# Four small edits in a kernel for delta attention and two gated layers: two more weight loads ahead of a marked point, one matrix product moved in the order, the last copies cut in two, one table load moved

## The chip, the cores and the metric

The kernel runs on one core of a Trainium2 chip. The metric is the device time of one execution in microseconds (us); lower is better. TensorE is written PE here (PEld for its weight loads), VectorE is DVE, ScalarE is ACT, GpSimd is POOL, SyncE is SP. L934 means line 934 of the kernel before.

## The reference

Three stages, one after the other, all in float32 (the inputs of the two layers come as float64 and are read as pairs of 32-bit words):

```python
# attention: q, k, v of (4, 8, 768, 48), beta of (4, 8, 768); a state of 48 x 48 for each head
for t in range(S):
    y[:, :, t] = q_t @ state
    state += beta_t * outer(k_t, v_t - state.T @ k_t)       # k_t normalised
x = y.transpose(0, 2, 1, 3).reshape(3072, 384)
# layer 1, d_ff = 1536
g = x @ w_gate
x = (g * sigmoid(g) * (x @ w_val)) @ w_out
# layer 2, d_ff = 2048
h = x @ w_in
out = np.where(h > 0, h, exp(min(h, 0)) - 1) @ w_out
```

## The kernel before

**Attention** is done in 12 groups g of 256 tokens. For a group SP loads k, q and v (`loads`: L447, L453, L460), `prepare` normalises k, makes transposes and products of k and q, and `invert` solves a small triangular system with many short DVE instructions (L673, L679) that end in a transpose (L687). `attention` then makes products on PE: `xstep` (L772, evicted by `xput`, L777), `gstep` (L792, evicted by `put`, L801), the chain over the state (L828) and the output (L862), transposed into `xh` and `xl` (L892, L895), the two parts of the input to layer 1.

**Layer 1** (`moe1`) runs over 12 blocks f of 128 columns for each group. A block is two projections on PE (L1028; gate, then value), Silu of the gate on ACT (`silu`, L1035), a product on DVE (L1038), its split into two parts (`hi` on ACT, L1042; `lo` on DVE, L1045) and the output product (`prod`, L1054), summed in `acc`. Results go through memory (`x2d`) to layer 2.

**Layer 2** (`moe2`) runs over 6 pairs of groups n and 16 blocks f each. A block is the projection `h2` (L1140, nine products), then `e0` Relu, `e1` Exp and `e2` on ACT (L1146, L1149, L1152), `e3`, `hi` and `lo` on DVE (L1155, L1160, L1163), then `out2` for four token tiles t (L1177), three products each. Tiles t = 0 and 1 are summed in the two halves of `acc`, t = 2 and 3 in two further banks (`at`). After the last block of a pair `ev` copies each tile out of its bank (L1190; even t on DVE, odd t on ACT) and `snd` issues its store on SP (L1194).

**Weights.** Layer 1 has 18 weight tiles w0 to w17: w0 and w1 hold gate and value columns of f = 0 and f = 1, w2 the output rows of both, w3 and w4 the columns of f = 2 and 3, w5 their rows, and so on. `load_w` issues one tile as two or four transfers on SP (L934 for columns, L931 for rows; 786,432 bytes a tile). `decode` turns a tile into two float32r parts in six passes over 128x768: `lowbits` (L954, ACT), `mag` (L960, ACT), the sign (`sign16` on ACT, L965, or `sign32` on DVE, L968, whichever the planner gives it to), `both` (L972, DVE), `hi` (L982, ACT) and `lo` (L986, DVE).

**The order** of all instructions is made by a planner (`Order`) when the program is built. Every step has costs for the engines that can do it, a priority (a lower number goes first) and the steps that it follows; the planner plays the program through and writes each engine's queue in the order of its own times. On the chip an engine takes its queue strictly in order and waits only where data or a buffer is not ready. Step `after=` is only a rule for the planner. A weight tile's load has priority 1 + n and the loads of the second group have 2.5. From tile number AHEAD on, a load may be planned only behind `mark[PAUSE]`, which is the last `xput` of the first group:

```python
load_w(n, src1(n), 1 + n, [] if n < AHEAD else [mark[PAUSE], sent[n - 2]])
```

Where the planner sees PE without work before its time 170 us, it puts in products that nothing reads: `fill` (L1207, 128x512), `quick` (L1213) and, in layer 1, `fill2` (L1218, 128x256). `h2` of a block has priority f within its pair, `out2` has f + 2, so that `h2` of block f + 1 precedes `out2` of block f, and `out2` of block f precedes `h2` of block f + 2.

Of the kernel before, what the change touches and what calls it, by code (L numbers as in the profile page):

```python
# [245 lines left out]
def delta_moe_kernel(ctx: ExitStack, tc: tile.TileContext, q, k, v, beta,  # L246
# [14 lines left out]
    ND = 10  # L261
    UNTIL = 170e3
    JOIN = (4,)
    AHEAD = 3
    PAUSE = (0, 'x')
    HOLD = (0, 'm')
    WARM = 8
# [72 lines left out]
    def act(n, f, psum=True):  # L340
        return [("ACT", (75 if psum else 110) + .8333 * n, (165 if psum else 190) + .8333 * n, 0, f)]
# [4 lines left out]
    def pe(ns, f, kind=0, n=18):  # L346
        return [("PE", ns, ns + 160, (kind, n), f)]
# [10 lines left out]
    P_MOE = 0.0  # L358
# [649 lines left out]
    def moe1(g, p):  # L1008
        xk = [("xh", g % 2, 0), ("xh", g % 2, 1), ("xl", g % 2, 0), ("xl", g % 2, 1),
              f"xh{g % 2}", f"xl{g % 2}"]  # L1010
        ev = None
        for f in range(F1):
            m, o = divmod(f, 2)
            wk = [f"w{3 * m + o}", f"w{3 * m + o}b"]
            ok = [f"w{3 * m + 2}", f"w{3 * m + 2}b"]
            h, hh = Slots(GV, 1), Slots(HB, 1)
            ht = Slots(TBS, 1)
            c = {}

            def proj(j, f=f, h=h):  # L1020
                def x():
                    dst = bank[h.got[0]][:, j * TB:(j + 1) * TB]
                    wt = w1(f, j)
                    n = 0
                    for a_, b_ in PASS:
                        xx = (xh, xl)[b_][g % 2]
                        for kk in range(KD):
                            PE.matmul(dst, lhsT=wt[:, a_, kk * 128:(kk + 1) * 128], rhs=xx[:, kk, :],  # L1028
                                      start=(n == 0), stop=(n == 3 * KD - 1))
                            n += 1  # L1030
                return x

            def silu(h=h, ht=ht, c=c):
                c['s'] = TT(ht.got[0], [128, TB])
                A.activation(out=c['s'], in_=bank[h.got[0]][:, 0:TB], func=ACTF.Silu)  # L1035

            def times(h=h, c=c):
                V.tensor_tensor(out=c['s'], in0=bank[h.got[0]][:, TB:2 * TB], in1=c['s'], op=ALU.mult)  # L1038

            def hi(hh=hh, c=c):  # L1040
                c['h'] = TT(hh.got[0], [128, 2, TB], F32R)
                A.copy(out=c['h'][:, 0, :], in_=c['s'])  # L1042

            def lo(e, c=c):
                return lambda: e.tensor_tensor(out=c['h'][:, 1, :], in0=c['s'],  # L1045
                                               in1=c['h'][:, 0, :].bitcast(F32), op=ALU.subtract)

            def prod(f=f, c=c):
                od.fill = fill2
                w = w1(f, 2)  # L1050
                for n, (a_, b_) in enumerate(((0, 0), (1, 0), (0, 1))):
                    for d in range(KD):
                        o_ = acc[:, d // 2, (d % 2) * TB:(d % 2) * TB + TB]
                        PE.matmul(o_, lhsT=w[:, a_, d * 128:(d + 1) * 128], rhs=c['h'][:, b_, :],  # L1054
                                  start=(f == 0 and n == 0 and d != 1), stop=(f == F1 - 1 and n == 2),
                                  skip_group_check=True)
            pp = p + f
            mark.setdefault((g, 'm'), add(pp, pe(1080, proj(0), 1), r=xk + wk, w=[(h, 0)], need=[h]))
            add(P_MOE, act(256, silu), r=[(h, 0)], w=[ht], need=[ht], use=[h])
            add(pp, pe(1080, proj(1), 1), r=xk + wk, w=[(h, 1)], use=[h])  # L1060
            add(P_MOE, dve(256, times), r=[(h, 1)], w=[ht], use=[h])
            after = buf.get(('evac', g - 1), ()) if f == 2 else ()
            add(P_MOE, act(256, hi, False), r=[ht], w=[(hh, 0)], need=[hh], use=[ht], after=after)
            add(P_MOE, dve(256, lo(V)), r=[ht, (hh, 0)], w=[(hh, 1)], use=[ht, hh])
            add(pp + 1.5, pe(1080, prod, 1), r=[(hh, 0), (hh, 1)] + ok, w=["acc"], use=[hh])
        buf['evac', g] = []
        for d0, d1 in ((0, 2), (2, KD)):
            h = Slots(HB, 1)
            c = {}

            def take(d0=d0, d1=d1, h=h, c=c):
                c['t'] = TT(h.got[0], [128, d1 - d0, TB])
                A.copy(out=c['t'], in_=acc[:, d0 // 2, 0:(d1 - d0) * TB].rearrange(
                    "p (d t) -> p d t", t=TB))

            def send(d0=d0, d1=d1, c=c):
                nc.sync.dma_start(out=x2d[g, :, d0:d1, :], in_=c['t'])
            buf['evac', g].append(add(P_MOE, act((d1 - d0) * TB, take), r=["acc"], w=[h], need=[h]))
            add(0, dma(131072 * (d1 - d0), send), r=[h], w=[("x2d", g, d0)], use=[h])
# [47 lines left out]
    def moe2(n, f, p, obs):  # L1127
        h, hr = Slots(H4, 1), Slots(HB, 1)
        tag = ("kp", "qp", "ain")[cnt["hs"] % 3]
        cnt["hs"] += 1  # L1130
        c = {}
        wk = [f"w{f}", f"w{f}b"]
        xk = [(x, n % 2, d) for x in ("x2h", "x2l") for d in range(KD)]

        def h2():
            x = bank[h.got[0]]
            m = 0
            for a_, b_ in PASS:
                for kk in range(KD):
                    PE.matmul(x, lhsT=W[f][:, 0, a_, kk * 128:(kk + 1) * 128], rhs=x2[n][b_][:, kk, :],  # L1140
                              start=(m == 0), stop=(m == 3 * KD - 1))
                    m += 1

        def e0():
            c['r'] = TT(hr.got[0], [128, TB2])
            A.activation(out=c['r'], in_=bank[h.got[0]], func=ACTF.Relu, scale=-1.0)  # L1146

        def e1():
            A.activation(out=c['r'], in_=c['r'], func=ACTF.Exp, scale=-1.0)  # L1149

        def e2():
            A.activation(out=c['r'], in_=c['r'], func=ACTF.Identity, bias=neg1, scale=1.0)  # L1152

        def e3():
            V.scalar_tensor_tensor(out=c['r'], in0=bank[h.got[0]], scalar=0.0, in1=c['r'],  # L1155
                                   op0=ALU.max, op1=ALU.add)

        def hi():
            c['h'] = TT(tag, [128, 2, TB2], F32R)
            V.tensor_copy(c['h'][:, 0, :], c['r'])  # L1160

        def lo():
            V.tensor_tensor(out=c['h'][:, 1, :], in0=c['r'], in1=c['h'][:, 0, :].bitcast(F32),  # L1163
                            op=ALU.subtract)
        add(p, pe(2100, h2, 1), r=xk + wk, w=[h], need=[h],
            after=buf['evac', NB - 1] if n == 0 and f > 1 else ())
        add(P_MOE, act(512, e0), r=[h], w=[hr], need=[hr], use=[h])
        add(P_MOE, act(512, e1, False), w=[hr])
        add(P_MOE, act(620, e2, False), w=[hr], r=["neg1"])
        add(P_MOE, dve(512, e3), r=[h], w=[hr], use=[h])  # L1170
        add(P_MOE, dve(256, hi), r=[hr], w=HS[tag], use=[hr])
        add(P_MOE, dve(512, lo), r=[hr] + HS[tag], w=[(tag, "lo")], use=[hr])
        for t in range(4):
            def out2(t=t):
                o = bank[obs[t].got[0]][:, 0:DM]
                for m, (a_, b_) in enumerate(PASS):
                    PE.matmul(o, lhsT=c['h'][:, b_, t * 128:(t + 1) * 128], rhs=W[f][:, 1][:, a_, :],  # L1177
                              start=(f == 0 and m == 0), stop=(f == F2 - 1 and m == 2))
            add(p + 2, pe(530, out2, 1, 6), r=wk + HS[tag] + [(tag, "lo")], w=[obs[t]],
                need=[obs[t]] if f == 0 else [], wait=["acc"] if n == 0 and f == 0 else [])  # L1180
        if f == F2 - 1:
            for t in range(4):
                ot = ("xh1", "xl1", "y0", "y1")[cnt["os"] % 4]
                cnt["os"] += 1
                ok = [ot] + ([(ot[:2], 1, 0), (ot[:2], 1, 1)] if ot[0] == "x" else [])
                d = {}

                def ev(t=t, ot=ot, d=d):
                    d['o'] = TT(ot, [128, DM])
                    (A.copy if t % 2 else V.tensor_copy)(out=d['o'], in_=bank[obs[t].got[0]][:, 0:DM])  # L1190

                def snd(t=t, d=d):
                    r0 = t * S + n * 128
                    nc.sync.dma_start(out=out[r0:r0 + 128, :], in_=d['o'])  # L1194
                add(P_MOE, (act if t % 2 else dve)(384, ev), r=[obs[t]], w=ok, use=[obs[t]])
                add(0, dma(196608, snd), r=ok)

# [104 lines left out]
```

## Time and profile before

| | |
|---|---|
| median of 3 runs | 1166.56 us (1163.58 to 1168.1) |
| profiled execution: its time, its span | 1167.36 us, 1165.7 us |
| mean granted clock of PE, share of full speed | 0.985 |
| PE busy | 1123.9 us, 96% of the span |
| DVE, ACT, POOL busy | 812.3 us (70%), 560.8 us (48%), 44.3 us (4%) |

The profile is one execution; all times in it count from the start of its span. A busy PE also counts the products that nothing reads.

### The profile page before, as it was taken

The page shows a single profiled execution, that of the slowest core. Times are in us where ns is not written, and L with a number is a line of the kernel's source. Part 1 is how long each engine was busy: PE and PEld are TensorE (multiplying, and loading weights), DVE is VectorE, ACT ScalarE, POOL GpSimd, SP SyncE. Part 2 cuts the span into 40 slices and gives each one's busy share as a digit, 9 for nine tenths or more (in the row PEclk, how much of TensorE's full clock was granted, in tenths as well). Part 3 has the DMA queues.
Part 4 walks back from the last instruction along what each step waited for, and adds up shares of the span by engine and source line. Part 5 has one row for each costly group of instructions (what it writes and reads, how often), then busy time and mean ns, then how long its engine had stood idle before and what let it go on. Part 6 is the DMA issues. An engine that isn't in the chain of part 4 may idle for free.

```text
span 1165.7 us, 34386 instructions
## 1 busy us (share of the span) xinstructions
PE 1123.9 (96%) x14728; PEld 1032.0 (89%) x14728; DVE 812.3 (70%) x2489; ACT 560.8 (48%) x1099; POOL 44.3 (4%) x57
## 2 busy tenths in 40 slices
PE   8889999999999999999999999999999999999997
PEld 6689988989899989998999898988888888888886
DVE  7889867878887878788878765995545444454443
ACT  7688442333333333334333434995545454454443
POOL 0100010100000000000000000000000000000000
PEclk9799999999999999999999999999999999999999
DMA  7770202020202020203020105900101001010000
GB/s 156 235 214 16 43 14 45 11 49 8 50 9 50 9 50 9 50 5 54 9 50 6 26 3 168 334 15 19 55 1 55 1 14 42 1 37 1 28 1 28
DMA packets 107625, 57.36 MB, mean 49 GB/s; under 512 B 77744, under 2 KB 102320, under 8 KB 107472
## 3 DMA queue, kind: packets, MB, share of 16 engines
q1 hardware_dynamic: 107472, 55.16, 17.9%
q8 instruction: 115, 1.88, 0.7%
q14 instruction: 38, 0.31, 0.1%
HBM read 45.71 MB, written 9.44 MB: 47 GB/s over the span
## 4 chain that ended last, share of the span: by engine, by line
PE 80%; DVE 12%; ACT 4%; issue 3%; DMA 0%; POOLq 0%; DVEq 0%; ACTq 0%
PE gv L1028 24%; PE acc L1054 10%; PE acc L1177 8%; PE at L1177 8%; PE at L1140 8%; PE gv L1140 8%; PE at L828 2%; PE at L792 2%; PE at L772 2%; PE at L598 1%; PE at L557 1%; PE acc L1207 1%; DVE hb L1045 1%; PE at L862 1%; DVE ain L642 1%
## 5 line engine op out<-in xcount | busy, mean ns | idle before, releaser
L1028 PE MATMUL gv<-xh,w 128*128 128x256 f32 x1728 | 291.5, 289 | 5.9 <-ACT xh L892 2.4
L1028 PEld LDWEIGHTS gv<-xh,w 128*128 128x128 f32 x1728 | 242.5, 194 | 12.2 <-ACT xh L892 3.1
L1054 PE MATMUL acc<-hb,w 128*128 128x256 f32 x1296 | 183.5, 287 | 1.2 <-ACT hb L1042 0.6
L1054 PEld LDWEIGHTS acc<-hb,w 128*128 128x128 f32 x1296 | 165.6, 192 | 5.0 <-ACT hb L1042 1.2
L1035 ACT ACTIVATE tb<-gv 128x256 f32<-128x256 f32 x144 | 55.3, 384 | 233.6 <-PE gv L1028 233.2
L1028 PE MATMUL gv<-xl,w 128*128 128x256 f32 x864 | 152.8, 286 | 3.3 <-DVE xl L895 3.2
L1028 PEld LDWEIGHTS gv<-xl,w 128*128 128x128 f32 x864 | 125.9, 194 | 4.4 <-DVE xl L895 4.0
L1038 DVE TENSOR_TENSOR tb<-gv,tb 128x256 f32<-128x256 f32 x144 | 60.3, 419 | 67.1 <-ACT tb L1035 54.7
L1042 ACT CAST hb<-tb 128x256 fp32r<-128x256 f32 x144 | 58.6, 407 | 87.9 <-DVE tb L1038 87.6
L1155 DVE SCALAR_TENSOR_TENSOR hb<-gv,hb 128x512 f32<-128x512 f32 x48 | 33.2, 691 | 94.3 <-ACT hb L1152 94.3
L1155 DVE SCALAR_TENSOR_TENSOR hb<-at,hb 128x512 f32<-128x512 f32 x48 | 33.2, 691 | 82.6 <-ACT hb L1152 82.6
L657 DVE TENSOR_TENSOR ain<-z,ain 128x60 f32<-128x60 f32 (+32 forms) x522 | 88.7, 208 | 2.5
L664 DVE TENSOR_TENSOR z<-z,ain 128x60 f32<-128x60 f32 (+32 forms) x522 | 88.7, 208 | 1.0
L1045 DVE TENSOR_TENSOR hb<-tb,hb 128x256 fp32r<-128x256 f32 x144 | 65.5, 455 | 14.7 <-ACT hb L1042 13.7
L1146 ACT ACTIVATE hb<-gv 128x512 f32<-128x512 f32 x48 | 28.7, 599 | 97.2 <-PE gv L1140 97.1
L1152 ACT ACTIVATE hb<-hb,neg 128x512 f32<-128x512 f32 x96 | 69.5, 724 | 3.0
L1146 ACT ACTIVATE hb<-at 128x512 f32<-128x512 f32 x48 | 28.7, 598 | 80.1 <-PE at L1140 79.8
L1149 ACT ACTIVATE hb<-hb 128x512 f32<-128x512 f32 x96 | 60.8, 633 | 2.9
L792 PE MATMUL at<-gr,R 32*96 32x80 f32 x1480 | 46.4, 255 | 1.0 <-issue 1.0
L792 PEld LDWEIGHTS at<-gr,R 32*96 32x96 f32 x1480 | 38.7, 163 | 7.8 <-ACT tb L1035 0.8
L1177 PE MATMUL acc<-w,ain 128*128 128x384 f32 x192 | 39.7, 340 | 1.7 <-DVE ain L1160 1.3
L1177 PE MATMUL acc<-w,kp 128*128 128x384 f32 x192 | 39.5, 339 | 1.6 <-DVE kp L1160 1.3
(209 smaller groups left out, 2090.0 us busy)
## 6 DMA issues: line engine op xcount, KB each, us to landing
w<-in_moe_w_out_dram SPq DMA_DIRECT2D x28, 384.0 KB, 6.7
w<-in_moe_w_in_dram SPq DMA_DIRECT2D x16, 384.0 KB, 5.8
w<-in_moe_w_gate_dram SPq DMA_DIRECT2D x12, 384.0 KB, 7.4
w<-in_moe_w_val_dram SPq DMA_DIRECT2D x12, 384.0 KB, 7.8
qp<-in_q_dram SPq DMA_DIRECT2D x11, 384.0 KB, 5.8
kp<-in_k_dram SPq DMA_DIRECT2D x11, 384.0 KB, 5.2
x2d<-hb SPq DMA_DIRECT2D x12, 256.0 KB, 2.0
R<-in_v_dram SPq DMA_DIRECT2D x24, 96.0 KB, 2.2
```

The source lines that it names most:

```text
L657: V.tensor_tensor(out=t, in0=z[:, l:l + 1, x:y].to_broadcast([128, m, y - x]), in1=an[:, l + 1:32, l:l + 1].to_broadcast([128, m, y - x]), ...
L664: V.tensor_tensor(out=z[:, l + 1:32, x:y], in0=z[:, l + 1:32, x:y], in1=t, op=ALU.add)
L792: PE.matmul(bank[h[c].got[0]][0:96, s * 80:s * 80 + 80], lhsT=R[t, u, :], rhs=gr[t, u, 0:80], start=True, stop=True, skip_group_check=True)
L1028: PE.matmul(dst, lhsT=wt[:, a_, kk * 128:(kk + 1) * 128], rhs=xx[:, kk, :], start=(n == 0), stop=(n == 3 * KD - 1))
L1038: V.tensor_tensor(out=c['s'], in0=bank[h.got[0]][:, TB:2 * TB], in1=c['s'], op=ALU.mult)
L1045: return lambda: e.tensor_tensor(out=c['h'][:, 1, :], in0=c['s'], in1=c['h'][:, 0, :].bitcast(F32), op=ALU.subtract)
L1054: PE.matmul(o_, lhsT=w[:, a_, d * 128:(d + 1) * 128], rhs=c['h'][:, b_, :], start=(f == 0 and n == 0 and d != 1), stop=(f == F1 - 1 and n ...
L1140: PE.matmul(x, lhsT=W[f][:, 0, a_, kk * 128:(kk + 1) * 128], rhs=x2[n][b_][:, kk, :], start=(m == 0), stop=(m == 3 * KD - 1))
L1149: A.activation(out=c['r'], in_=c['r'], func=ACTF.Exp, scale=-1.0)
L1152: A.activation(out=c['r'], in_=c['r'], func=ACTF.Identity, bias=neg1, scale=1.0)
L1155: V.scalar_tensor_tensor(out=c['r'], in0=bank[h.got[0]], scalar=0.0, in1=c['r'], op0=ALU.max, op1=ALU.add)
L1177: PE.matmul(o, lhsT=c['h'][:, b_, t * 128:(t + 1) * 128], rhs=W[f][:, 1][:, a_, :], start=(f == 0 and m == 0), stop=(f == F2 - 1 and m == 2))
```

## The change

Four edits. (1) AHEAD goes from 3 to 5: w3 and w4 may be planned ahead of the marked point. (2) In layer 1, behind the Silu of the last block of the last group, ACT gets an Exp of a 128x1 tile whose result is not used, planned at 1400 ns. (3) `h2` of the last block of the last pair gets a priority lower by 0.5, so that it precedes `out2` of block 13. (4) In the last pair each tile's copy out of its bank is two copies of 192 columns, the first on DVE and the second on ACT, and the store follows both.

```diff
-    AHEAD = 3
+    AHEAD = 5
...
             add(P_MOE, act(256, silu), r=[(h, 0)], w=[ht], need=[ht], use=[h])
+            if g == NB - 1 and f == F1 - 1:
+                add(P_MOE, [("ACT", 1400.0, 1500.0, 0, lambda: A.activation(
+                    out=sm[2][:, 0:1], in_=neg1, func=ACTF.Exp))], r=["neg1", ht], w=["sm"])
...
-        add(p, pe(2100, h2, 1), r=xk + wk, w=[h], need=[h],
+        add(p - (0.5 if n == NB // 2 - 1 and f == F2 - 1 else 0), pe(2100, h2, 1), r=xk + wk, w=[h], need=[h],
             after=buf['evac', NB - 1] if n == 0 and f > 1 else ())
...
-                def ev(t=t, ot=ot, d=d):
-                    d['o'] = TT(ot, [128, DM])
-                    (A.copy if t % 2 else V.tensor_copy)(out=d['o'], in_=bank[obs[t].got[0]][:, 0:DM])
+                parts = 2 if n == NB // 2 - 1 else 1
+                w_ = DM // parts
+                for x in range(parts):
+                    def ev(t=t, x=x, ot=ot, d=d, w_=w_):
+                        if x == 0:
+                            d['o'] = TT(ot, [128, DM])
+                        (A.copy if (t if parts == 1 else x) % 2 else V.tensor_copy)(
+                            out=d['o'][:, x * w_:x * w_ + w_], in_=bank[obs[t].got[0]][:, x * w_:x * w_ + w_])
+                    e = (act if (t if parts == 1 else x) % 2 else dve)
+                    add(P_MOE, e(w_, ev), r=[obs[t]] + (ok if x else []), w=[("o", t, x)] + ([] if x else ok),
+                        use=[obs[t]])
...
-                add(P_MOE, (act if t % 2 else dve)(384, ev), r=[obs[t]], w=ok, use=[obs[t]])
-                add(0, dma(196608, snd), r=ok)
+                add(0, dma(196608, snd), r=ok + [("o", t, x) for x in range(parts)])
```

## Rows read from the trace of the kernel before

**Rows 1.** Page, part 1: busy time, share of span, instructions.

```profile
PE 1123.9 (96%) x14728; PEld 1032.0 (89%) x14728; DVE 812.3 (70%) x2489; ACT 560.8 (48%) x1099; POOL 44.3 (4%) x57
```

**Rows 2.** Busy time by stretch; columns: stretch, length, engines, PE clock, DMA share, GB/s.

```profile
15.00:20.00 5.00, 5.00 (x62) 3.93 (x62) 4.35 (x20) 3.73 (x6) 0.00 (x0) 1.00 1.03 268
20.00:25.00 5.00, 3.50 (x146) 2.81 (x148) 4.59 (x16) 5.00 (x5) 0.00 (x0) 0.93 0.01 2
...
24.00:58.00 34.00, 28.88 (x785) 22.69 (x774) 28.53 (x52) 23.31 (x41) 3.50 (x3) 0.76 0.73 212
58.60:125.00 66.40, 62.56 (x1232) 58.45 (x1230) 62.05 (x125) 54.62 (x92) 3.88 (x3) 0.97 0.37 100
```

**Rows 3.** The same for L1218 alone (products nothing reads), 0 to 180 us, the sum.

```profile
sum 180.00, PE 7.09 PEld 6.31; mean PE 0.20 PEld 0.18
```

**Rows 4.** Chain that ended last, 78 to 93 us: start, length, what.

```profile
80.61 0.91 ACT w L954
81.53 0.84 ACT w L982
```

**Rows 5.** Timeline of SP: start, length, line, tile and source, count.

```profile
25.79 0.38 SPq L447 DMA_DIRECT2D kp<-in_k_dram  x1
26.22 1.30 SPq L934 DMA_DIRECT2D w<-in_moe_w_gate_dram  x1
```

**Rows 6.** Waits of SP, 0 to 150 us: total us, times, longest.

```profile
SPq L447 <- DVE gr L546: 13.0, 1, 13.0
```

**Rows 7.** Timeline of PE around the first group's xstep.

```profile
33.96 0.76 PE L772 MATMUL at<-gr,ain 32*32 32x80 f32 x25 [3.52 <-issue]
```

**Rows 8.** Waits of DVE, 24 to 58 us.

```profile
DVE gr L777 <- PE at L772: 1.9, 2, 1.0
DVE lc L801 <- PE at L792: 1.0, 2, 0.8
DVE w L986 <- ACT w L982: 1.0, 1, 1.0
```

**Rows 9.** Instructions of L968 on DVE: times in ns (min/median/max), first and last start.

```profile
L968 DVE SCALAR_TENSOR_TENSOR w<-w x25: 942/951/960, 48.4 to 782.1; 128x768 int32<-128x768 int32 x25
```

**Rows 10.** Timeline of ACT, 72 and 86 us: Silu of blocks 3 and 4.

```profile
72.29 0.39 ACT L1035 ACTIVATE tb<-gv 128x256 f32<-128x256 f32 x1
...
86.87 0.39 ACT L1035 ACTIVATE tb<-gv 128x256 f32<-128x256 f32 x1 [0.48 <-PE gv L1028]
```

**Rows 11.** Chain that ended last, 750 to 765 us.

```profile
756.77 0.75 ACT hb L1073 x2
...
757.54 1.28 ACT L1149
...
758.83 0.64 ACT hb L1149
```

**Rows 12.** Waits of PE, 740 to 800 us.

```profile
PE acc L1177 <- DVE kp L1160: 1.3, 1, 1.3
```

**Rows 13.** ACT by form: copy of 192 columns, function of one column.

```profile
L840 ACT COPY sv<-at 48x192 f32<-48x192 f32 x3 | 0.9, 317 | 0.1
L1227 ACT ACTIVATE sm<-neg 128x1 f32<-128x1 f32 x1 | 0.2, 203 | 0.0
```

**Rows 14.** Timeline of PE from 1155 us.

```profile
1157.81 0.44 PE L1177 MATMUL acc<-w,ain 128*128 128x384 f32 x1 [1.26 <-DVE ain L1160]
1158.54 1.14 PE L1177 MATMUL acc<-w,ain 128*128 128x384 f32 x5 [0.28 <-DVE ain L1163]
```

**Rows 15.** Instructions of L1190, the whole run, and who waited.

```profile
  DVE xh L1190: 5.7, 6
```

**Rows 16.** Timeline from 1159 us: copies and stores.

```profile
1159.72 0.56 DVE L1190 COPY xh<-acc 128x384 f32<-128x384 f32 x1 [1.23 <-PE acc L1177]
...
1160.77 0.48 ACT L1190 COPY y<-at 128x384 f32<-128x384 f32 x1
1161.24 0.91 SPq L1194 DMA_DIRECT2D out_dram<-y  x2
```

## Prediction

> **What bounds the kernel now.** I read the page's first part, then busy time by stretch, then the chain of waits in the three places that the diff touches. PE is busy 96% of the span and DVE 70% [rows 1], so as a whole PE sets the time, and an edit on DVE or ACT pays only where PE is idle or turns products that nothing reads. There are three such places. From 58.6 to 125 us, while the 18 weight tiles of layer 1 are decoded, PE is idle for 66.40 - 62.56 = 3.8 us and spends 7.1 us on `fill2`, while DVE is busy 62.05 of 66.40 us: DVE is the bound there [rows 2, 3]. The chain of waits says with what: passes of `decode` [rows 4], and Silu of block 3 comes at 72.3, that of block 4, which needs w6, only at 86.9 [rows 10]. The second place is the start of layer 2, where PE waits 1.3 us for the first `out2` [rows 12]. The third is the end: behind `out2` of block 14 PE waits 1.26 and 0.28 us for the split of block 15 [rows 14].
>
> **Edit 1, AHEAD.** It adds and removes no instruction; it moves transfers. First what the pause is: on SP nothing waits for the last `xput`. w3 is issued at 26.22, right behind k of group 2 (counting from 1), and it is this k load that stood for 13.0 us, until DVE had read the old k [rows 5, 6]; `xput` is later, since its products end after 33.96 [rows 7]. So the queue becomes: w0 to w4 with no wait, then q and k of the second group, then w5 and w6 at about 26.2, where w3 and w4 were. q goes out later by four issues; nobody reads it before the k of its group, which stands behind the same wait as before. Five transfers of 786 KB then run into the quiet stretch: DMA moves 268 GB/s from 15 to 20 us and 2 GB/s from 20 to 25 [rows 2]; two tiles at 268 GB/s are 1.57 MB / 268 = 5.9 us, so w3 lands near 22 to 23 and w4 near 25.5. That costs the path nothing visible: what hides it is that DMA had 5 us without work. The 3.52 us in which PE waits for nothing that the profile shows lie beside the transfers issued at 26.2 [rows 5, 7]; w5 and w6 now take that place, so I leave the stall.
>
> What comes of it: `decode` of w3 and w4 can start some 20 us earlier than now, when the first of its sign passes on DVE is at 48.4 [rows 9]. A tile wants two or three passes of 0.951 us on DVE, so the two tiles 3.8 to 5.7 us. In 24 to 58 us DVE has 34 - 28.5 = 5.5 us free [rows 2]. Not all of that holds a pass: three waits are 1.0 us long, and one 0.8 [rows 8]. I take three passes, 2.9 us. Bounds: 0, if the planner's own times show no gap there, and 5.5 us, all that is free. Below 0 it goes too (the rival further down). What DVE does early it needn't do after 58.6, where it is the bound, and PE has 3.8 + 7.1 = 10.9 us of idle time and unread products to give up. So -2.9 us.
>
> **Edit 2, the table.** The load is 1.28 us between a copy that ends at 757.52 and the first Exp at 758.83 [rows 11], on the chain to the first `out2`, for which PE waits 1.3 us [rows 12]. Moved up to the last Silu it comes before work of lower priority (three decode passes), which then stands behind it; ACT has no gap there, so the load is not hidden by idle time, only exchanged with those passes. The added Exp of one column is 0.2 us, by the row of the Sqrt of that shape [rows 13]. Bounds: -1.3 (the wait is gone) and +0.2 (the planner pushes everything back by the load, and the passes still go first). I take -1.1, near the first, since products of layer 1 and 2 have priority 0 on ACT and decode has 500 and more. If the passes pushed back are late for block 3 of layer 2, part comes back; that is in the bound.
>
> The Trainium skill (ScalarE: Activation LUTs, What ACT_TABLE_LOAD costs) puts a switch at 1283 ns for the load and some 1380 ns of drain, 2.66 us in all. By it this edit would give up to 2.5 us, and the sum would be 1.4 us lower. The trace agrees on the load and shows no drain: from the end of the copy to the first Exp are 1.31 us.
>
> **Edit 3, `h2` of block 15.** PE's order at the end is now `h2` 14, `out2` 13, `h2` 15, `out2` 14, wait, `out2` 15. It becomes `h2` 14, `h2` 15, `out2` 13, 14, 15. The chain of block 15 on ACT and DVE starts 2.1 us earlier (one `out2` of four tiles), and I take both engines to be free for it: ACT is busy 48% and DVE 70% of the span [rows 1]. The product before the wait ended at 1157.81 - 1.26 = 1156.55; the bulk of the last `out2` starts at 1158.54 with one product of twelve done [rows 14]. Without the wait it starts at 1156.55 and has twelve: 1158.54 - 1156.55 = 2.0 us less. Bounds: 0 (the planner's times keep the old order) and -2.1 (all of one `out2`). I take -2.0.
>
> **Edit 4, the copies.** Now the last copy is 0.48 us on ACT at 1160.77, and the two last stores are issued from 1161.24 [rows 16]. A copy of 192 columns on ACT is 0.32 us [rows 13]; DVE's 0.56 cut in the same ratio is 0.37. Two halves at once would end the last copy some 0.1 us earlier. But they read one bank. In all six pairs ACT's copy from `acc` sat until DVE's copy from `acc` had ended (5.7 us in six times), and those were even two banks of one tile [rows 15]. So the halves go in turn: for t = 0 and 1 a chain of 0.37 + 0.32 + 0.37 + 0.32 and hops, 1.45 us from 1159.7; then t = 2 and 3, whose last half ends near 1161.8 instead of 1161.25. SP's spacing of about 0.45 us between stores hides half of that. Bounds: -0.1 and +0.6. I take +0.3.
>
> The Trainium skill (PSUM — Partial Sum Buffer, PSUM bank collisions raise a hardware error) says that two engines, ACT and DVE too, must not touch one bank in the same quadrant of partitions at once, and that accesses there are kept apart; different banks run clean. It speaks against this edit. By it only the halves of one tile go in turn, which gives +0.2 in the place of +0.3; the trace shows the turn even between the two banks of `acc`.
>
> **The sum**, against the profiled execution of 1167.36 us (1165.7 of span and 1.7 around it): -2.9 - 1.1 - 2.0 + 0.3 = -5.7, so 1161.7. That execution lies 0.8 us above the median, so the median becomes 1166.56 - 5.7 = 1160.9 us, 0.49% less. Its own range: 1158.5 to 1163.
>
> **Rivals.** (A) Edit 1 gives nothing: the planner sees no gap ahead of 58 us, or PE's stalls move elsewhere. For it: DVE's gaps are there because PE stood for 3.52 us [rows 7, 8], and the planner may not know of that stall. Against: ACT has 34 - 23.3 = 10.7 us free there [rows 2]. It gives -2.8, 1163.8 us. (B) Edit 1 gives all that DVE has free, 5.5 us, or more, if block 4 moves up in the place of `fill2` and PE's clock, 0.97 in that stretch [rows 2], no longer dips: -5.5 - 2.8 = -8.3, 1158.3 us; PE's 10.9 us give the far end, 1152.9. For it: block 4 waits 14 us for w6 [rows 10]. Against: half of DVE's gaps are shorter than a pass. (C) Slower: the twelve passes of w3 and w4 stand in ACT's and DVE's queues ahead of the first group's copies, and a queue goes in order, so that a pass that waits for its weights to land, or that has just begun, holds `xput`, `put` and the state's chain behind it, and PE, which idles meanwhile, has its lower clock for longer (0.76 of full speed in 24 to 58 us [rows 2], 1.2 GHz being half). Twelve passes of 0.9 us [rows 4, 9], all on the path, are +10.8 - 2.8 = +8.0, 1174.6 us; from ten passes on (+9.0 - 2.8 = +6.2) it is slower by over 0.5%. Against: the 3.52 us stall covers the first three or four.
>
> **Chances.** A time within 0.5% (5.8 us) of before can't be told from no change here, as the three runs before already differ by 0.4%. The forecast sits on that bound: 0.40, of it 0.21 beyond it. A 0.24 (within). B 0.23 (faster). C 0.13: 0.10 slower, 0.03 within, when fewer than ten passes are on the path. Faster 0.21 + 0.23 = 0.44, same 0.19 + 0.24 + 0.03 = 0.46, slower 0.10. The range leaves out the far end of B (0.08) and most of C (0.11): 1155.0 to 1167.0.
>
> **What would show it.** Edit 1: SP issues five tiles before the k load of 25.8 us; `lowbits` of w3 before 26 us; Silu of block 4 well before 86.9; less than 7.1 us of L1218. It is wrong if `xput` or the first Silu of layer 1 come later by more than 3 us. Edit 2: a table load near 752 at L1060 or so, none at 757.5, and no wait of 1.3 us at the first `out2`. Edit 3: two projections in a row at the end and no wait at the last `out2`. Edit 4: the ACT halves begin when the DVE halves end. The total is wrong if PE's idle time between 125 and 740 us changes by more than 3 us, for the planner writes that stretch anew as well, and nothing in the diff says which way.

## The result and the profile after

The changed kernel takes 1143.53 us (median of 6 executions, 1140.05 to 1148.89), the kernel before beside it 1163.11 (6 executions, 1160.88 to 1168.1). The ratio is 0.9833 (95% interval 0.9806 to 0.9860): 19.6 us less, where the forecast had 5.7 and its range reached down to 1155. The profiled execution took 1148.89 us, the slowest of its six.

Part 1 of the page of the changed kernel, which answers to [rows 1]:

```profile
PE 1116.3 (97%) x14711; PEld 1027.4 (90%) x14711; DVE 808.2 (70%) x2489; ACT 562.0 (49%) x1104; POOL 43.3 (4%) x57
```

The span fell by 1165.7 - 1147.2 = 18.5 us: PE's idle time from 41.8 to 30.9 us, its busy time by 7.6. Where that lies is seen best when the span is cut at three marks, the first Silu of the second group, the last Silu of layer 1, and the end:

| | to first Silu of group 2 | from there to last Silu of layer 1 | layer 2 and the end |
|---|---|---|---|
| before | 130.4 | 621.3 | 414.0 |
| after | 125.5 | 612.7 | 409.0 |
| difference | -4.9 | -8.6 | -5.0 |

I call the second column the stretch. No edit adds, removes or changes an instruction in it.

**First column.** SP's timeline in the changed kernel, against [rows 5]:

```profile
12.02 0.43 SPq L934 DMA_DIRECT2D w<-in_moe_w_gate_dram  x1
12.49 0.58 SPq L934 DMA_DIRECT2D w<-in_moe_w_val_dram  x1
13.19 0.55 SPq L453 DMA_DIRECT2D qp<-in_q_dram  x1
13.78 7.50 SPq L934 DMA_DIRECT2D w<-in_moe_w_gate_dram  x1
21.33 0.84 SPq L934 DMA_DIRECT2D w<-in_moe_w_val_dram  x1
27.65 0.37 SPq L447 DMA_DIRECT2D kp<-in_k_dram  x1
```

w3 goes out at 12.0 and w4 at 13.8, ahead of the k load, as forecast (q stands between them). What was not: the issue of w4's first half held SP for 7.5 us. Busy time by stretch, against [rows 2], with its columns (the engines in the order of [rows 1]):

```profile
24.00:58.00 34.00, 27.52 (x815) 20.87 (x815) 31.01 (x56) 24.63 (x42) 3.46 (x3) 0.85 0.65 195
58.60:125.00 66.40, 62.73 (x1267) 58.73 (x1266) 61.73 (x132) 57.37 (x97) 3.55 (x3) 1.00 0.35 95
```

DVE does 31.01 - 28.53 = 2.5 us more in 24 to 58 us. `lowbits` of w3 on ACT begins at 23.0 us, where it was 43.4. The sign passes on DVE, against [rows 9], begin 17 us earlier:

```profile
L968 DVE SCALAR_TENSOR_TENSOR w<-w x24: 945/952/1807, 31.4 to 770.0; 128x768 int32<-128x768 int32 x24
```

Silu of blocks 3 and 4 on ACT, against [rows 10]: the gap of 14.6 us is one of 7.

```profile
74.04 0.47 ACT L1035 ACTIVATE tb<-gv 128x256 f32<-128x256 f32 x1
81.00 0.38 ACT L1035 ACTIVATE tb<-gv 128x256 f32<-128x256 f32 x1 [0.20 <-PE gv L1028]
```

The products that nothing reads (`fill2`, now L1228), against [rows 3]:

```profile
sum 180.00, PE 4.50 PEld 3.93; mean PE 4.50 PEld 3.93
```

**The stretch.** Busy time by stretch, kernel before (columns as in [rows 2]), then the changed kernel:

```profile
130.37:751.64 621.27, 601.12 (x10344) 569.13 (x10343) 488.83 (x1890) 242.52 (x596) 34.62 (x39) 0.99 0.19 47
```

```profile
125.48:738.20 612.72, 599.30 (x10353) 569.06 (x10352) 486.69 (x1897) 240.88 (x593) 34.10 (x39) 0.99 0.19 46
```

The work is nearly the same: 9 products more on 10,344, and 2.1 us less of DVE. PE's idle time falls from 621.27 - 601.12 = 20.2 to 13.4 us. Waits of PE between 125 and 735 us (total, times, longest; `issue` is idle time for which the profile shows no wait), before:

```profile
PE gv L1028 <- DVE xl L895: 3.2, 4, 1.2
PE gv L1028 <- ACT xh L892: 2.4, 3, 1.3
PE at L598 <- issue: 2.1, 2, 1.5
```

and after:

```profile
PE at L598 <- issue: 2.7, 2, 1.9
PE gv L1028 <- issue: 2.0, 2, 1.0
...
PE gv L1028 <- DVE xl L895: 0.7, 1, 0.7
```

In the kernel before PE stood 5.6 us, in seven waits, for `xh` and `xl`, the input of a group that attention had only just finished. Afterwards 0.7 us of that is left.

**Layer 2.** ACT in the changed kernel around the moved table load, against [rows 11]:

```profile
738.20 0.39 ACT L1035 ACTIVATE tb<-gv 128x256 f32<-128x256 f32 x1 [0.22 <-PE gv L1028]
738.61 1.28 ACT L1061 ACT_TABLE_LOAD   x1
739.90 0.20 ACT L1061 ACTIVATE sm<-neg 128x1 f32<-128x1 f32 x1
...
743.88 0.65 ACT L1152 ACTIVATE hb<-hb 128x512 f32<-128x512 f32 x1
```

The first Exp (L1152) follows with no load ahead of it, and of the 1.3 us that PE waited [rows 12] there is left, in 738 to 760 us:

```profile
PE acc L1180 <- DVE kp L1166: 0.2, 1, 0.2
```

PE's timeline at the end, against [rows 14]: two projections in a row (1132.11 to 1136.46), and no wait from there to the last product.

```profile
1132.11 0.85 PE L1143 MATMUL gv<-R,w 128*128 128x512 f32 x3
...
1135.60 0.86 PE L1143 MATMUL gv<-R,w 128*128 128x512 f32 x3
1136.30 1.22 PE L1180 MATMUL acc<-w,kp 128*128 128x384 f32 x6
...
1141.54 1.21 PE L1180 MATMUL at<-w,ain 128*128 128x384 f32 x6
```

The last copies on DVE, then on ACT, against [rows 16]:

```profile
1141.74 0.36 DVE L1197 COPY xh<-acc 128x192 f32<-128x192 f32 x1 [1.24 <-PE acc L1180]
1142.48 0.36 DVE L1197 COPY xl<-acc 128x192 f32<-128x192 f32 x1 [0.39 <-ACT xh L1197]
1142.76 0.61 DVE L1197 COPY y<-at 128x192 f32<-128x192 f32 x2
```

```profile
1142.13 0.32 ACT L1197 COPY xh<-acc 128x192 f32<-128x192 f32 x1 [3.61 <-DVE xh L1197]
1142.88 0.32 ACT L1197 COPY xl<-acc 128x192 f32<-128x192 f32 x1 [0.42 <-DVE xl L1197]
1143.14 0.58 ACT L1197 COPY y<-at 128x192 f32<-128x192 f32 x2
```

The four halves from `acc` go strictly in turn. The last copy ends 1.0 us behind the last product, where it was 0.5.

### The profile page after: what moved, and what is told of

It is laid out like the page before. It is cut to its first block, busy times and chain, and to the rows that moved or that the text cites. A ratio compares the mean times of both kernels' runs of the same rounds, so it can differ in the third digit from the quotient of the medians.

```text
span 1147.2 us, 34358 instructions
## 1 busy us (share of the span) xinstructions
PE 1116.3 (97%) x14711; PEld 1027.4 (90%) x14711; DVE 808.2 (70%) x2489; ACT 562.0 (49%) x1104; POOL 43.3 (4%) x57
## 4 chain that ended last, share of the span: by engine, by line
PE 86%; DVE 8%; ACT 4%; issue 2%; DVEq 0%; ACTq 0%
PE gv L1028 26%; PE acc L1054 12%; PE acc L1180 9%; PE at L1180 9%; PE gv L1143 9%; PE at L1143 8%; PE at L792 3%; PE at L828 3%; PE at L557 2%; PE at L772 2%; PE at L598 2%; PE at L862 1%; PE acc L1217 1%; DVE sv L834 1%; ACT tb L1035 1%
## 5 line engine op out<-in xcount | busy, mean ns | idle before, releaser
L1045 DVE TENSOR_TENSOR hb<-tb,hb 128x256 fp32r<-128x256 f32 x144 | 63.2, 439 | 14.4 <-ACT hb L1042 12.8
L1152 ACT ACTIVATE hb<-hb 128x512 f32<-128x512 f32 x96 | 60.9, 634 | 2.9
L1143 PE MATMUL gv<-lc,w 128*128 128x512 f32 x144 | 41.2, 394 | 0.0
L1143 PE MATMUL at<-lc,w 128*128 128x512 f32 x144 | 40.9, 394 | 0.0
```

## The experiments

Ratios are to the kernel before on the same chip, with 95% intervals. The theory at first (L): DVE's lead from the first group is handed on, so that later groups find xh and xl ready. The rival (C): the planner wrote another order for the stretch, which happens to be better.

**Which edit.** e1 is the kernel before with the first edit alone, e2 the changed kernel without it, e4 the changed kernel without the split copies (so with edits 1 to 3). In e3 the order of before is kept and SP only issues w3 and w4 right behind w2; in it w3 and w4 of layer 1 get the bytes of layer 2's tiles of those numbers.

```diff
e1  -    AHEAD = 3
    +    AHEAD = 5
e2  -    AHEAD = 5
    +    AHEAD = 3
e4  -                parts = 2 if n == NB // 2 - 1 else 1
    +                parts = 1
e3  +        late[n] = f
    +        def g():
    +            if n < 3 or n > 4:
    +                f()
    +            if n == 2:
    +                late[3]()
    +                late[4]()
```

e1: 

> The kernel before with AHEAD = 5 and nothing else. Theory P (plan): AHEAD makes the planner write another order on every engine up to some 700 us, and the new order is the gain, also after the 18 tiles are decoded. By the stage lengths of the two profiles it is worth 5.5 + 5.0 + 3.6 - 0.6 = 13.5 us: ratio 0.988, and 8 or 9 of these us lie after 125 us. Theory D (decode): only the two tiles decoded early count, 5 us, ratio 0.9955, and the rest of the 18.5 us comes from edits 2 to 4.

e2: 

> The kernel after with AHEAD back at 3: edits 2, 3 and 4 alone. Theory P: the stage lengths give 1.5 us at the start of layer 2, 3.0 us up to the end of the products and 0.5 us behind them, 4 to 5 us in all: ratio 0.996, and up to 700 us the profile looks as that of before. Theory D: 13 us, ratio 0.989.

e3: 

> The kernel before with the planner's order of PE, ACT, DVE and POOL unchanged; only SP issues the transfers of w3 and w4 right behind those of w2, so that they land 20 us earlier while nothing uses them earlier. Theory P: the order is the gain, so no change, ratio 0.999 to 1.001. Theory D: no change either, as decode stays where it is in the queues. A third theory (contention: fewer transfers beside PE's stall of 3.5 us at 30 us and beside the chain of the first group): 2 to 4 us, ratio 0.997.

e4: 

> The kernel after without edit 4: the last copies whole, in turn on DVE and ACT. All theories: the split costs some 0.3 us at the end, so the ratio is that of the kernel after (0.983) less 0.0003, which can't be told by time; in the profile the last copy ends 0.5 us after the last product and not 1.0 us.

Measured: e1 0.9866 (0.9837 to 0.9895), 15.6 us less; e2 0.9956 (0.9938 to 0.9974), 5.1 us less; e3 1.000 (0.9979 to 1.0022); e4 0.9819 (0.979 to 0.9847), 1143.03 us against 1143.53 with the split. The microseconds are from the ratios. So the edits add up within the intervals, as theory P had it, four fifths of the gain are the first edit's, the split copies neither give nor take anything that can be measured, and early transfers alone are worth nothing: without the planner's new order the passes keep their places (the first sign pass on DVE is at 47.6 us in e3, at 48.4 before).

**Is the order a matter of chance?** Two numbers of the planner's own cost model are shifted a little, in the kernel before (p1, p2) and after (p3, p4).

```diff
p1, p3  -    HOP = 40.0
        +    HOP = 44.0
p2, p4  -    def lag(l, n=45.0):
        +    def lag(l, n=50.0):
```

p1: 

> The kernel before with a planner constant changed that has nothing to do with the weights (the time it adds from one engine to another, 44 ns in the place of 40). No transfer is moved; only the order of steps that tie in the planner. Theory L (lead: the time that DVE gains before 58 us is carried on from group to group): ratio 0.997 to 1.003. Theory C (chance: any new order is worth up to 10 us either way, and AHEAD = 5 drew a good one): anywhere from 0.985 to 1.015, as likely as not beyond 0.995 or 1.005.

p2: 

> The kernel before with another such constant (the time behind a short DVE instruction of the triangular system, 50 ns in the place of 45). Theory L: 0.997 to 1.003. Theory C: anywhere from 0.985 to 1.015.

p3: 

> The kernel after with the constant of p1. Theory L: as the kernel after, 0.980 to 0.987. Theory C: the good draw is lost, nearer to 0.996 (edits 2 to 4 alone) than to 0.983 as likely as not.

p4: 

> The kernel after with the constant of p2. Theory L: 0.980 to 0.987. Theory C: as for p3.

Measured: p1 0.9979 (0.9954 to 1.0005), p2 0.994 (0.9917 to 0.9963), p3 0.9837 (0.9788 to 0.9886), p4 0.9861 (0.9808 to 0.9914). The gain outlasts other orders, as L had it, but p2 lies outside what L allowed: an order alone is worth up to 0.6%.

**More or less work for DVE, known to the planner.** d1 (changed kernel) and d2 (before) add passes, d3 (before) leaves some out, d4 (changed kernel) sets AHEAD to 4.

```diff
d1, d2  +        if not isinstance(tag, tuple) and 5 <= n < 11:
        +            add(p, [("DVE", 960.0, 1060.0, 0, lo(V))],
        +                r=tkeys + [key], w=[keyb])
d3      -            add(p, [("DVE", 955.0, 1020.0, 0, sign32), ("ACT", 1940.0, 1990.0, 0, sign16)],
        -                r=[key, keyb], w=[(key, "lo")])
        +            if isinstance(tag, tuple) or not 5 <= n < 11:
        +                add(p, [("DVE", 955.0, 1020.0, 0, sign32), ("ACT", 1940.0, 1990.0, 0, sign16)],
        +                    r=[key, keyb], w=[(key, "lo")])
```

d1: 

> The changed kernel, and in layer 1 the last decode pass (DVE, 0.95 us) of w5 to w10 is done twice, with the same result: six passes, 5.7 us, more work for DVE between 58 and 125 us, of which the planner gives some 2 us away by moving sign passes to ACT. Theory L (lead): what DVE is ahead or behind by in that stretch decides whether xl and xh of the next groups are ready when PE wants them, so a loss there is paid again at the starts of the later groups: 8 to 16 us more in all, 1152 to 1159, and the waits of the gate projection for xl and xh between 125 and 735 us are back at 3 us or more. Rival C (the new plan happened to fall well): the loss is paid once, at most 5.7 us, 1144 to 1149, and those waits stay near 0.7 us.

d2: 

> The same six doubled passes in the kernel before. Theory L: the first stage is longer by 2 to 5.7 us and the later groups by more of the same, 5 to 14 us in all, 1168 to 1177. Rival C: at most 5.7 us, 1163 to 1169.

d3: 

> The kernel before, its transfers as they were, with the sign pass of w5 to w10 of layer 1 left out (these tiles lose the signs of their weights; nothing else is left out): five passes of 0.95 us less on DVE, 4.75 us, and one of 1.9 us less on ACT. It gives DVE the lead by other means than the earlier loads. Theory L: 9 to 14 us less than before, 1149 to 1154, with the waits for xl and xh between 125 and 735 us falling from 5.6 us to under 2. Rival C: 4 to 6 us less, 1157 to 1159, those waits as before. A third theory, that only w3 and w4 in memory early can do it: nothing to 5 us.

d4: 

> The changed kernel with AHEAD 4: only w3 is asked for ahead of the mark. Theory L: about half of the gain of the two tiles is left, so 1149 to 1153 (1143.5 with both, 1159 with none). Rival C: anything between 1143 and 1159, not in order.

Measured: d1 1156.88 us, 0.9938 (0.9913 to 0.9962); d2 1156.38, 0.9953 (0.9933 to 0.9974); d3 1158.71, 0.9963 (0.9943 to 0.9984); d4 1163.43, 0.9984 (0.9958 to 1.001). d1's time is L's, but its waits for xl and xh stay at 1.0 us, as C had it, and the loss lies in the first column (first Silu of group 2 at 133.0 us). d2 speaks against L: with six passes more the kernel before gets faster, its stretch 621.3 to 612.7 us (some 5 of these 8.6 us are time at the lower clock, see the table below); it lies below C's range too. d3 gains what C said, though its order is another one too, and those waits fell to 1.7 us, as L said. d4 is slower than either theory had it: none of the gain is left, not even that of edits 2 to 4. Its first Silu comes at 64.7 us, against 61.0, and that of group 2 at 133.7, against 130.4. As every one of these kernels has an order of its own, they can't separate the theories.

**The same order, more or less work.** Now the planner is told nothing, so that the sequence on every engine stays as it was, but for the passes added or left out (s2 and s4 leave out sign passes, so their results lack the signs of those weights).

```diff
s1, s3  -            return lambda: e.tensor_tensor(out=W[n][:, :, 1, :], in0=c['f'],
        -                                           in1=W[n][:, :, 0, :].bitcast(F32), op=ALU.subtract)
        +            def f():
        +                for _ in range(2 if not isinstance(tag, tuple) and 5 <= n < 11 else 1):
        +                    e.tensor_tensor(out=W[n][:, :, 1, :], in0=c['f'],
        +                                    in1=W[n][:, :, 0, :].bitcast(F32), op=ALU.subtract)
        +            return f
s2, s4  +            skip = not isinstance(tag, tuple) and 5 <= n < 11
        -            add(p, [("DVE", 955.0, 1020.0, 0, sign32), ("ACT", 1940.0, 1990.0, 0, sign16)],
        +            add(p, [("DVE", 955.0, 1020.0, 0, (lambda: None) if skip else sign32),
        +                    ("ACT", 1940.0, 1990.0, 0, (lambda: None) if skip else sign16)],
```

s1: 

> The changed kernel with its order of instructions kept: the last decode pass of w5 to w10 is issued twice inside its step, of which the planner knows nothing, 6 x 0.95 = 5.7 us of DVE in the first group. Stretch from the first Silu of the second group to the last Silu of layer 1, 612.7 us in the changed kernel: under L the lead is gone and it goes to 618 us or more, and the whole to 1154 or more; under C it stays at 611 to 615 and the whole gets at most 5.7 us longer, 1145 to 1149.

s2: 

> The kernel before with its order kept, and the sign passes of w5 to w10 of layer 1 left out (those tiles lose the signs of their weights): three passes of 0.95 us less on DVE and three of 1.9 us less on ACT in the first group. The same stretch, 621 us before: under L it falls to 616 or less and the whole by 8 us or more, to 1155 or less; under C it stays at 619 to 623 and the whole falls by 2 to 5 us, 1158 to 1161.

s3: 

> The kernel before with its order kept and the last decode pass of w5 to w10 issued twice, 5.7 us more of DVE in the first group. Under L the stretch goes from 621 to 625 or more and the whole to 1171 or more; under C the stretch stays at 619 to 623 and the whole is at most 5.7 us longer, 1164 to 1169. With the six passes known to the planner the whole had become 7 us shorter, and the stretch 8.6.

s4: 

> The changed kernel with its order kept and the sign passes of w5 to w10 left out (those tiles lose the signs of their weights): three passes less on DVE, three less on ACT. Both theories: the whole falls by 2 to 5 us through the first group. Under L the stretch may fall below 610 us; under C it stays at 611 to 615.

Measured: s1 1150.05 us, 0.9871 (0.9832 to 0.991); s2 1163.17, 0.9993 (0.9972 to 1.0014); s3 1168.95, 1.0043 (1.002 to 1.0065); s4 1145.32, 0.9827 (0.9782 to 0.9871). The added passes cost about once what they last, 4 to 7 us for 5.7 (s1 ends 1 us above C's range, 4 below L's); those left out give nothing that can be measured, where both theories had 2 us or more. The stretch tells the theories apart. Busy time by stretch of s1 (late by 5.7 us of DVE, order of the change):

```profile
129.90:739.70 609.80, 596.34 (x10353) 566.05 (x10351) 486.27 (x1897) 240.38 (x593) 34.03 (x39) 1.00 0.19 46
```

It begins 4.4 us later than in the changed kernel and is not longer: L had 618 us or more, C 611 to 615. s2's stretch, 615.7 us, is by its number what L had (616 or less), but its profile has only 3.4 us at the half clock in it where the kernel before has 13.7; with half of that time taken out the two are 614.0 and 614.4. All kernels side by side, worked out from such rows (one profile each; the time at half clock is from the trace's clock records; kernels of the first two lines have the same sequence on PE, DVE and ACT in the stretch):

| order in the stretch | kernels | stretch, us | PE idle in it | at half clock in it | stretch less half of that |
|---|---|---|---|---|---|
| of before | before, e2, e3, s2, s3 | 615.7 to 622.8 | 18.8 to 20.5 | 3.4 to 17.1 | 613.3 to 615.5 |
| of the change | after, e1, e4, s1, s4 | 609.8 to 612.7 | 13.3 to 14.1 | 3.4 to 13.7 | 605.9 to 608.1 |
| others, AHEAD 3 or 4 | p1, p2, d2, d3, d4 | 612.7 to 617.2 | 16.2 to 20.8 | 3.4 to 17.1 | 606.9 to 612.4 |
| others, AHEAD 5 to 7 | p3, p4, d1, s5, s6 | 604.3 to 613.4 | 10.8 to 17.7 | 0 to 10.2 | 602.6 to 609.2 |

That half of the time at half clock is lost is an estimate; the order of before bears it out, with 615.7 us at 3.4 us of it (s2) and 622.8 at 17.1 (e3). The last column moves by some 2 us for one order, whatever stands ahead of it, and by up to 12 us from order to order. By it the order of before is the slowest of all that ran.

**How many tiles.** The changed kernel with AHEAD 6 (s5) and 7 (s6).

```diff
s5, s6  -    AHEAD = 5
        +    AHEAD = 6     (s6: 7)
```

s5: 

> The changed kernel with AHEAD 6. If the number of tiles sets the time, w5 early is no worse than w3 and w4: 1138 to 1146, first Silu of the second group at 126 us or earlier. If each order is a draw of its own: anywhere in 1140 to 1160, the stretch from there to the last Silu of layer 1 between 607 and 615 us with the time at the lower clock taken out.

s6: 

> The changed kernel with AHEAD 7. By the number of tiles 1136 to 1146, still earlier than with 6; as a draw 1140 to 1160, not in order with 4, 5 and 6.

Measured: s5 1141.92 us, 0.9806 (0.9764 to 0.9848); s6 1142.05, 0.9814 (0.9778 to 0.9849). Neither can be told from AHEAD 5. The first Silu of group 2 comes at 127.6 and 127.1 us, later than after the change; the stretch makes up for it. Busy time by stretch of s5:

```profile
127.56:731.86 604.30, 593.54 (x10344) 564.26 (x10343) 486.01 (x1890) 239.87 (x592) 34.18 (x39) 1.00 0.19 47
```

Its 10,344 products are as many as in the kernel before, with 9.4 us less idle time of PE between them.

## Why the prediction was wrong, step by step

**Edit 1, the transfers: right.** Five tiles went out ahead of the k load, w5 and w6 took the place behind it, and DMA was quiet again by about 25 us. SP's issue took longer than thought (7.5 us), which cost nothing that shows: behind it stood w4's second half and the k load, and that load waited for DVE until 27.6 anyway. The stall ahead of `xstep` [rows 7] became 2.4 us, with 1.3 and 1.0 in two other waits beside it.

**Edit 1, the term of -2.9: mis-sized.** DVE did take 2.5 us more into 24 to 58 us, near the three passes forecast. But the first column fell by 4.9 us in the changed kernel and by 7.3 in e1 (to 123.0). Three kernels of each order have nothing added or left out ahead of the stretch: before, e2 and e3 with 130.4, 129.1 and 127.5 us, after, e1 and e4 with 125.5, 123.0 and 123.1, so 5.1 us less in the mean, with 2 to 3 us between profiles of one order. That is the size of rival B, and what B named came with it: block 4 moved up by 5.9 us, `fill2` fell by 2.6, and the clock in 58.6 to 125 us is 1.00 in place of 0.97. The forecast weighed only DVE's free time. The clock does not decide: in e3 3.4 us of this column are at the half clock, in the kernel before 20.5, and e3 is only 2.9 us shorter. Work also left the first group: up to the first Silu of group 2 DVE is busy 113.8 us before and 109.9 after. That the bound there is not DVE alone is seen in s2, where passes taken out of a fixed order gave nothing; what holds it then was not tried.

**The step that failed: the sum held nothing for 125 to 740 us.** The prediction named this as what would make its total wrong, said that nothing in the diff shows the sign, and put zero, with no width for it in the range. It was the largest term. By the five kernels of each order the stretch is 619.4 us in the mean before and 610.9 after: -8.5, of it 6.2 PE's idle time (19.8 to 13.6), and, by the estimate above, some 1.4 from less time at the half clock (10.2 to 7.5 us). The s runs show that this comes with the order and not with a lead on the chip. So do the waits for `xh` and `xl`: between 125 and 735 us all five kernels of the order of before have seven of them, 5.3 to 5.9 us, and all five of that of the change have one, 0.7 us, s1 with its six passes more too. That is 5 of the 6.2 us. It is no rule for other orders: d4 has only 0.2 us of these waits and the longest idle time of all, 14.1 us of it `issue`. How much of it any other order would have given is told less sharply: with AHEAD 3 or 4, five other orders average 610.6 us in the last column of the table, against 614.3 for that of before and 607.2 for that of the change, so about half of the 7 us is luck, in that the order of before was a poor one. The five others with AHEAD 5 to 7 average 606.6. Why the planner packs that stretch better with the tiles early, in p3, p4, d1, s5 and s6 too, stays open.

**Edits 2 to 4: right in kind, small by 1.2 us.** Layer 2 and the end take 411.6 to 414.6 us in nine kernels without them (mean 413.3) and 408.9 to 410.1 in eleven with them (409.3; e4, without the split copies, 409.2): -4.0 against -1.1 - 2.0 + 0.3 = -2.8. The traces say where, if layer 2 is cut at the first Relu of its second pair and of its last (medians of the nine and the eleven). From the last Silu of layer 1 to the first cut it is 71.5 and 69.8 us, from there to the second 267.8 in both, and from there to the last product 69.1 and 67.0. So edit 3 gave its 2.0 us, and the term that was mis-sized is edit 2's: -1.8 in the place of -1.1, beyond its bound of -1.3. The wait of 1.3 us is gone; where the other 0.5 lies stays open. The Trainium skill (ScalarE: Activation LUTs, What ACT_TABLE_LOAD costs) adds a drain to the load; here 1.28 us of load are followed at once by the Exp, at 739.90.

**Edit 4: the mechanism was right.** ACT's halves from `acc` begin when DVE's end, and DVE's next half, in the other bank of `acc`, waits for ACT's. The Trainium skill (PSUM — Partial Sum Buffer, PSUM bank collisions raise a hardware error) has only accesses to one bank in turn; the two tiles `at` agree, ACT copying one from 1143.14 us while DVE copies the other until 1143.37. In `acc` the turn goes across both banks; the trace names the other engine's copy as what each half waited for, and whether the chip would need that no run shows. The price of +0.3 can't be told in the whole: from the last product to the end it is 3.8 to 5.1 us in the ten kernels with whole copies and 4.4 to 5.3 in the ten with halves.

## What to carry to other kernels

Where a program plans its instructions, a change of one number near the start rewrites everything behind it: give the part that no edit touches a width of its own, from a few kernels with the planner's costs shifted slightly (here up to 0.6% of the time), before a sum of microseconds is trusted. To tell a gain that is handed on from one that comes with the new order, change the work and keep the order. Compare stretches between marks that all kernels share, and, where PE sets the time, take what the lower clock costs out first.

## What the runs showed of the hardware

An issue on SP can hold the queue: in all ten kernels with AHEAD 5 to 7 that of w4's first half, behind w3 and q, took 6.81 to 8.43 us (7.50 in the changed kernel). With four tiles (d4) the longest issue of a weight there was 1.15 us. In e3, which also sends five tiles, but with layer 2's bytes for w3 and w4 and q behind them, those of w3 and w4 took 0.72 us at most. So the number of tiles is not enough; what holds the queue was not tried. The time at the half clock differs between executions of the same order: 3.4 to 17.1 us in the stretch, which goes with up to 7 us between two profiles (615.7 and 622.8). One dip, behind the small products and waits of attention; busy time by stretch of the kernel before, with the granted clock third from the end:

```profile
186.20:189.50 3.30, 2.35 (x136) 2.08 (x135) 3.23 (x11) 1.41 (x4) 0.17 (x1) 1.00 0.03 7
...
192.00:193.00 1.00, 1.00 (x6) 1.00 (x6) 0.95 (x4) 0.28 (x1) 0.00 (x0) 0.50 0.06 16
193.00:194.00 1.00, 1.00 (x7) 1.00 (x6) 1.00 (x9) 0.00 (x0) 0.00 (x0) 0.50 0.00 0
...
195.00:196.00 1.00, 1.00 (x10) 1.00 (x10) 0.00 (x0) 0.00 (x0) 0.00 (x0) 1.00 0.00 0
```

PE is busy 2.35 of 3.3 us at the full 2.4 GHz. From 192 to 194 us it runs at 1.2 GHz and gets 6 or 7 products a microsecond through; from 195, at 2.4 GHz again, 10.
